# A range test moved into the second layer, and a shorter conversion of the weights

## The chip, the cores and the metric

The kernel runs on one core of a Trainium2 chip. The metric is the device time of one execution in microseconds (us), the median of several executions. The engines are named as the profile names them: PE is TensorE (its weight loads are PEld), DVE VectorE, ACT ScalarE, POOL GpSimd, and SP issues DMAs.

## What is computed

A linear attention with a decaying state, and after it two feed-forward layers with squared ReLU. Cut to what matters:

```python
def _attn_ref(r, k, v, w, u):            # (4, 8, 768, 48) each, u (8, 48)
    state = np.zeros((B, H, D, D))
    for t in range(S):
        cur = np.einsum('bhd,bhe->bhde', u[None] * kt, vt)
        y[:, :, t] = np.einsum('bhd,bhde->bhe', rt, state + cur)
        state = wt[:, :, :, None] * state + np.einsum('bhd,bhe->bhde', kt, vt)

def _moe_ref(x, w_in, w_out):            # x (3072, 384), w_in (384, 2048)
    r = np.maximum(x @ w_in, 0.0)
    return r * r @ w_out                 # twice, with two sets of weights
```

The decays `w` lie between 0.8 and 0.95. The weights come as 64-bit floats, two 32-bit words each, and the device turns them into 32-bit floats.

## The kernel before

Attention is cut into 24 tiles of 128 tokens (`tile_ops`, L168). For each tile DVE makes two scans over the decays, G from the back (`scan_g`, L223) and F from the front (`scan_f`, L229). The products of keys and queries with them (`scaled`, L253) go to PE: transposes `kb` (L265, for the first six tiles also sums at L268), scores `sc` (L296, 32 small matmuls), `U` (L321), the output `y` (L365) and its transpose `xp` (L375). DVE carries the state from tile to tile (`Sp` at L330, `Sn` at L340), adds at L370 and writes the low half of the result, `xl` (L386), after ACT has written the high half `xh` (L379). All of these results share three PSUM buffers, the tag `ab`, taken in turn: the n-th takes the one that the result three before it has given up. Each buffer is given up by the engine that copies it out: that of `kb` by ACT at L278, that of `sc` by ACT at L299, those of `U` by DVE at L340, that of `xp` by DVE at L386.

The kernel is exact only while the decays' products stay in range. So for each tile ACT squares G and F and sums them into one column of `chk` (L257). A general, slow program runs instead if a test fails; with these inputs it does not.

The feed-forward layers take the tokens in blocks (`BLOCKS`, L31: in layer 1 512, 256, 256 and four times 512 tokens, in layer 2 six times 512). For each of the 16 chunks of 128 hidden channels PE makes nine matmuls `h` (L695; three times three, since each operand is split into a high and a low half), ACT takes ReLU and square (L702, L707), the result is split into `gh` and `gl` (L714, L720), and nine matmuls go to `acc` (L738). The first `h` needs block 0 whole: the four tiles 0 to 3. Tiles 4 and 5 are made while PE works on block 0, and so on.

A chunk of weights (`chunk_ops`, L441) is loaded in 768 KB (L451, three buffers `raw`) and converted in six steps: ACT takes the magnitude of the high words, scaled, and sums it for a test (L456); DVE shifts it (L459), puts the sign in (L462) and the top three bits of the low words (L465); ACT rounds the high half `whi` (L469), DVE makes the low half `wlo` (L472). Layer 1's 16 chunks are converted before and during block 0, layer 2's at the end of layer 1 and in layer 2's first block, and all stay in SBUF for their layer.

A planner sets the order of instructions on each engine at build time (`Order`, L58). Every step has a cost in a table, the results it needs, the buffers it takes and gives back, and a due time; the planner always takes the step that can begin first, and among those that can begin within 0.1 the one due first. On the chip each engine then runs its instructions in that fixed order and waits for what is late. Where PE would be idle in the plan ahead of the first `h`, `keep_warm` (L639) puts in matmuls whose result nobody reads.

Of the kernel before, what the change touches and what calls it, by code (L numbers as in the profile page):

```python
# [129 lines left out]
class Attn:  # L130
# [34 lines left out]
    def bank(self):  # L165
        return self.ps.tile([128, 512], F32, tag="ab", name="ab")

    def tile_ops(self, order, i, due, xdst):  # L168
# [48 lines left out]
        def scan_g():  # L217
            GF = t["GF"] = self.wp1.tile([QR, 2, SW + 1], F32, tag="GF", name="GF")
            t["G"], t["F"] = GF[:, 0], GF[:, 1]
            aend = t["aend"] = self.wp.tile([QR, SEG], F32, tag="aend", name="aend", bufs=4)  # L220
            Wt = parts()[0]
            nc.vector.memset(self.starts[:, 65::65], 1.0)
            nc.vector.tensor_tensor_scan(out=t["G"][:, 1:][:, ::-1], data0=Wt[:, 1:][:, ::-1], data1=self.starts[:, 1:][:, ::-1],  # L223
                                         initial=0.0, op0=ALU.mult, op1=ALU.add)
            nc.vector.tensor_scalar(out=aend, in0=t["G"][:, 1:SW:65], scalar1=LEAST, scalar2=None, op0=ALU.max)  # L225
            nc.vector.reciprocal(out=self.starts[:, 0:SW:65], in_=aend)

        def scan_f():
            nc.vector.tensor_tensor_scan(out=t["F"][:, 1:], data0=parts()[0][:, 0:SW], data1=self.starts[:, 0:SW],  # L229
                                         initial=0.0, op0=ALU.mult, op1=ALU.add)  # L230
# [660 lines left out]
```

## Time and profile before

| | us |
|---|---|
| median of 3 runs | 943.89 |
| lowest and highest | 942.64, 943.93 |
| the profiled execution | 946.26 |
| its span, first to last instruction | 944.5 |
| PE busy in the span | 925.4 |
| DVE busy | 533.0 |
| ACT busy | 458.2 |

The profiled execution is 2.4 us above the median, and 1.8 us of it lie outside the span. PE is busy for 98% of the span, but matmuls are pipelined and a matmul at half clock is as busy as one at full clock, so the share alone doesn't say what can be saved. Before the first `h` its busy time is also filled up by the keep-warm matmuls.

### The profile page before, as it was taken

To read this page: it belongs to the slowest core of one execution; us is meant where nothing else is said; L and a number is where in the kernel's file an instruction comes from. 1 tells how busy PE (TensorE), PEld (TensorE's weight loads), DVE (VectorE), ACT (ScalarE), POOL (GpSimd) and SP (SyncE) were. 2 spreads that over 40 slices of the span, in tenths; PEclk is the share of its full clock that TensorE was granted. 3 is DMA by queue.
4 is the path that set the end of the run, shared out by engine and by line. 5 is a ranking of instruction groups with operands and counts; after the bars stand their busy time and mean duration, and the time that the engine had idled before them with its cause. 6 is when DMAs were issued, how large, how long until landed. Compare 5 with 4: busy or idle time off the path is not lost.

```text
span 944.5 us, 16077 instructions
## 1 busy us (share of the span) xinstructions
PE 925.4 (98%) x6392; PEld 782.6 (83%) x6392; DVE 533.0 (56%) x897; ACT 458.2 (49%) x850; POOL 106.8 (11%) x123
## 2 busy tenths in 40 slices
PE   7898999999999999999999999999999999999997
PEld 7887889998887888888888888888888888888896
DVE  6799888787758484664433999532422422422322
ACT  4667866676554654555343676432333333322331
POOL 2201304043404123030100000000000000000000
PEclk8798999999999999999999999999999999999999
DMA  9556423233313413131022453120110200200201
GB/s 244 144 163 216 157 78 105 83 110 118 105 52 95 123 53 93 34 98 45 1 86 82 155 194 130 40 52 0 37 31 1 49 19 0 56 1 1 35 1 37
DMA packets 57444, 73.78 MB, mean 78 GB/s; under 512 B 35888, under 2 KB 44208, under 8 KB 57360
## 3 DMA queue, kind: packets, MB, share of 16 engines
q1 hardware_dynamic: 56944, 72.27, 26.5%
q8 instruction: 52, 0.85, 0.4%
q10 hardware_dynamic: 416, 0.40, 0.1%
q14 instruction: 32, 0.26, 0.1%
HBM read 63.21 MB, written 9.44 MB: 77 GB/s over the span
## 4 chain that ended last, share of the span: by engine, by line
PE 76%; DVE 0%; DMA 0%; ACT 0%; issue 0%; ACTq 0%
PE acc L738 35%; PE h L695 35%; PE ab L365 2%; PE ab L296 1%; PE ab L321 1%; PE ab L265 1%; PE ab L375 0%; DMA out_dram<-o 0%; DVE GF L223 0%; DVE gh L714 0%; DVE aend L225 0%; DVE o L754 0%; ACT o L754 0%; DVE gl L720 0%; PE ab L400 0%
## 5 line engine op out<-in xcount | busy, mean ns | idle before, releaser
L702 ACT ACTIVATE gf<-h 128x512 f32<-128x512 f32 (+1 forms) x208 | 117.3, 564 | 346.5 <-PE h L695 319.7
L714 DVE CAST gh<-gf 128x512 fp32r<-128x512 f32 (+1 forms) x192 | 82.6, 430 | 329.9 <-PE acc L738 282.7
L695 PE MATMUL h<-xh,whi 128*128 128x512 f32 (+1 forms) x624 | 238.0, 381 | 0.0
L695 PE MATMUL h<-xl,whi 128*128 128x512 f32 (+1 forms) x624 | 234.1, 375 | 0.0
L695 PE MATMUL h<-xh,wlo 128*128 128x512 f32 (+1 forms) x624 | 233.9, 375 | 0.0
L738 PE MATMUL acc<-gh,whi 128*128 128x512 f32 (+1 forms) x576 | 217.7, 378 | 0.8 <-DVE gh L714 0.8
L738 PE MATMUL acc<-gl,whi 128*128 128x512 f32 (+1 forms) x576 | 214.3, 372 | 1.3 <-DVE gl L720 1.2
L738 PE MATMUL acc<-gh,wlo 128*128 128x512 f32 (+1 forms) x576 | 214.2, 372 | 0.0
L720 DVE TENSOR_TENSOR gl<-gf,gh 128x512 fp32r<-128x512 f32 (+1 forms) x208 | 144.8, 696 | 8.7 <-ACT gh L714 1.2
L695 PEld LDWEIGHTS h<-xh,wlo 128*128 128x128 f32 x624 | 117.9, 189 | 21.1
L695 PEld LDWEIGHTS h<-xh,whi 128*128 128x128 f32 x624 | 117.9, 189 | 21.1
L695 PEld LDWEIGHTS h<-xl,whi 128*128 128x128 f32 x624 | 118.0, 189 | 20.7 <-DVE xl L386 1.1
L707 ACT ACTIVATE gf<-gf 128x512 f32<-128x512 f32 (+1 forms) x208 | 124.6, 599 | 6.5
L738 PEld LDWEIGHTS acc<-gl,whi 128*128 128x128 f32 x576 | 108.6, 189 | 20.3 <-DVE gl L720 2.1
L738 PEld LDWEIGHTS acc<-gh,whi 128*128 128x128 f32 x576 | 108.6, 188 | 20.4 <-DVE gh L714 1.0
L738 PEld LDWEIGHTS acc<-gh,wlo 128*128 128x128 f32 x576 | 108.4, 188 | 18.9
L303 POOL TENSOR_SCALAR_AFFINE_SELECT rs<-rs 64x512 f32<-64x512 f32 x48 | 35.9, 749 | 300.9 <-ACT rs L299 299.3
L333 ACT COPY sv<-Sp 64x192 f32<-64x192 f32 x88 | 30.6, 348 | 42.5 <-DVE Sp L330 41.5
L223 DVE TENSOR_TENSOR_SCAN GF<-wkr,starts 112x520 f32<-112x520 f32 x24 | 31.9, 1329 | 5.4 <-DMA wkr<-in_wkr_dram 2.2
L253 DVE TENSOR_TENSOR wkr<-wkr,GF 112x512 f32<-112x512 f32 x48 | 33.8, 729 | 0.0
L472 DVE SCALAR_TENSOR_TENSOR wlo<-c,whi 128x768 fp32r<-128x768 f32 x32 | 30.7, 962 | 4.7 <-ACT whi L469 4.3
L465 DVE SCALAR_TENSOR_TENSOR c<-raw,c 128x768 int32<-128x768 int32 x32 | 31.6, 986 | 0.7
(67 smaller groups left out, 832.7 us busy)
## 6 DMA issues: line engine op xcount, KB each, us to landing
raw<-in_w_dram SPq DMA_DIRECT2D x32, 768.0 KB, 4.3
wkr<-in_wkr_dram SPq DMA_DIRECT2D x23, 675.9 KB, 6.6
rk<-in_nat_dram SPq DMA_DIRECT2D x18, 384.0 KB, 4.9
vn<-in_nat_dram SPq DMA_DIRECT2D x24, 192.0 KB, 2.6
sv<-in_nat_dram SPq DMA_DIRECT2D x48, 96.0 KB, 2.6
x<-o SPq DMA_DIRECT2D x15, 256.0 KB, 2.1
xr<-x SPq DMA_DIRECT2D x15, 256.0 KB, 2.6
out_dram<-o SPq DMA_DIRECT2D x120, 32.0 KB, 1.6
```

Source lines behind the costliest of these rows:

```text
L223: nc.vector.tensor_tensor_scan(out=t["G"][:, 1:][:, ::-1], data0=Wt[:, 1:][:, ::-1], data1=self.starts[:, 1:][:, ::-1], initial=0.0, op0=A ...
L253: nc.vector.tensor_tensor(out=x, in0=x, in1=seg(t["GF"[n]], 1 - n), op=ALU.mult)
L303: nc.gpsimd.affine_select(out=x, in_=x, pattern=[[0, SEG], [1, C]], base=0, channel_multiplier=-1, compare_op=ALU.is_gt, fill=0.0)
L333: nc.scalar.copy(out=t["sv"][own[a], a, c::2], in_=t["Sp"][own[a]])
L465: nc.vector.scalar_tensor_tensor(out=t["c"], in0=t["low"], scalar=29, in1=t["c"], op0=ALU.logical_shift_right, op1=ALU.bitwise_or)
L472: nc.vector.scalar_tensor_tensor(out=t["hl"][1], in0=t["cf"], scalar=BACK, in1=t["hl"][0].bitcast(F32), op0=ALU.mult, op1=ALU.subtract)
L695: nc.tensor.matmul(out=h[:, 0:N], lhsT=a[:, cs], rhs=b[:, kk, 0:N], start=n == 0, stop=n == 8)
L702: nc.scalar.activation(out=g[:, 0:N], in_=hs.pop((l, j, f))[:, 0:N], func=AF.Relu)
L707: nc.scalar.activation(out=g[:, 0:N], in_=g[:, 0:N], func=AF.Square)
L714: copy(out=gh[:, 0:N], in_=g[:, 0:N])
L720: nc.vector.tensor_tensor(out=gl[:, 0:N], in0=g[:, 0:N], in1=gh[:, 0:N].bitcast(F32), op=ALU.subtract)
L738: nc.tensor.matmul(out=dst, lhsT=a, rhs=c, start=f == n == 0, stop=f == KF - 1 and n == 2)
```

## The change

Three things. First, for tiles 0 to 5 the square on ACT goes away (`TESTED_LATE = 6`). Their decays are loaded again in layer 2, G and F are scanned again, and ACT squares them there (`Attn.test_ops`). Second, the conversion of a chunk has five steps: ACT makes an integer of the top three bits of the low word out of its top byte, in place (`tail`), DVE joins it with the shifted high word and masks the sign in (`join`, two steps), ACT rounds, DVE subtracts. It has no test in it. Third, the test of the weights is made in layer 2: every chunk of both layers is loaded a second time, ACT takes the magnitude, and DVE counts in two steps what is too large and what too small (`Weights.test_ops`); chunk k's magnitude waits for the second load of chunk k+1. The last steps on `chk` move from layer 2's second block to its last. Due times change as well: tiles 0 and 1, 2 and 3, and the weights (6 instead of 12 ahead of their use). `HALVED` is 0, so the new passes over half a block do not occur.

```diff
-SCALE, BACK, LARGEST = 2.0 ** -111, 2.0 ** -8, 2.0 ** -96
+TESTED_LATE = 6
+HALVED = 0
...
-            pe_y=1.14, pe_x=0.45, magnitude=1.1, shift=0.56, top=0.96, tail=0.96, hi=0.83, lo=0.96, issue=0.4, warm=0.3)
+            pe_y=1.14, pe_x=0.45, word=0.83, join=0.96, hi=0.83, lo=0.96, issue=0.4, warm=0.3)
...
+    def test_ops(self, order, i, due):
...
+        add("SP", C_["issue"], load, "w again", [("x", NTILE - 1)], take=[("wkr", key)], moves=4 * QR * SW)
+        add("DVE", C_["scan"] + C_["ends"], scan_g, "G again", [("w again", i), ("F again", i - 1) if i else ("F", NTILE - 1)], take=[("GF", key), ("aend", key)], port=True)
+        add("DVE", C_["scan"], scan_f, "F again", [("G again", i)], port=True)
+        add("ACT", C_["square"], lambda: self.sum_squares(t, i), "chk", [("F again", i)], drop=[("GF", key), ("aend", key), ("wkr", key)])
...
         for n in range(2):
-            add("DVE", C_["product"], lambda n=n: scaled(n), ("kS", "rT")[n], ["GF"[n], whole] + (["rkT"] if by_pe else []), 0.14, port=True)
-        add("ACT", C_["square"], lambda: nc.scalar.activation(out=t["GF"][:, :, 1:], in_=t["GF"][:, :, 1:], func=AF.Square, accum_out=self.chk[0:QR, i:i + 1]),
-            "chk", ["kS", "rT"], 0.16, drop=[("GF", i)])
+            add("DVE", C_["product"], lambda n=n: scaled(n), ("kS", "rT")[n], ["GF"[n], whole] + (["rkT"] if by_pe else []) + (["kS"] if n else []), 0.14, port=True,
+                drop=[("GF", i)] if n and i < TESTED_LATE else ())
+        if i >= TESTED_LATE:
+            add("ACT", C_["square"], lambda: self.sum_squares(t, i), "chk", ["kS", "rT"], 0.16, drop=[("GF", i)])
...
         def tail():
-            nc.vector.scalar_tensor_tensor(out=t["c"], in0=t["low"], scalar=29, in1=t["c"], op0=ALU.logical_shift_right, op1=ALU.bitwise_or)
+            low = t["raw"][:, :, 0]
+            nc.scalar.activation(out=low, in_=t["raw"].bitcast(U8)[:, :, 3], func=AF.Copy, scale=1 / 32, bias=-15.5 / 32)
+
+        def join(n):
+            low, high = t["raw"][:, :, 0], t["raw"][:, :, 1]
+            if n == 0:
+                t["c"] = self.tmp_p.tile([128, 2 * DM], I32, tag="c", name="c")
+                nc.vector.scalar_tensor_tensor(out=t["c"], in0=high, scalar=3, in1=low, op0=ALU.logical_shift_left, op1=ALU.bitwise_or)
+            else:
+                nc.vector.scalar_tensor_tensor(out=t["c"], in0=high, scalar=0x3FFFFFFF, in1=t["c"], op0=ALU.bitwise_or, op1=ALU.bitwise_and)
...
+    def test_ops(self, order, k, due, chk):
...
+        def size():
+            t["a"] = self.tmp_p.tile([128, 2 * DM], I32, tag="c", name="c").bitcast(F32)
+            nc.scalar.activation(out=t["a"], in_=t["raw"][:, :, 1].bitcast(F32), func=AF.Abs)
...
+        order.add("SP", C_["issue"], load, ("raw2", k), [("issued", ("raw2", k - 1) if k else ("raw", 2 * KF - 1))], due=due, early=EARLY, take=[("raw", ("test", k))], moves=2048 * DM)
+        add("ACT", "word", size, "size", [("raw2", min(k + 1, 2 * KF - 1))], take=[("c", ("test", k))])
+        add("DVE", "join", lambda: count(0), "count0", [("size", k)], port=True)
+        add("DVE", "join", lambda: count(1), "count", [("count0", k)], port=True, drop=[("c", ("test", k)), ("raw", ("test", k))])
...
-        lo, hi = (at[number[0, j - 1, 0]], at[number[0, j, 0]]) if j else (0, BEGIN)
-        lo, hi = lo + (hi - lo) * p / n, lo + (hi - lo) * (p + 1) / n
+        if j:
+            lo, hi = at[number[0, j - 1, 0] if j > 1 else HALVED], at[number[0, j, 0]]
+            lo, hi = lo + (hi - lo) * p / n, lo + (hi - lo) * (p + 1) / n
+        else:
+            lo, hi = ((0, BEGIN), (BEGIN * 0.8, at[HALVED]))[p]
...
-        W.chunk_ops(order, k, at[number[k // KF, 0, k % KF]] - 12, A.chk)
+        W.chunk_ops(order, k, at[number[k // KF, 0, k % KF]] - 6)
+    for i in range(TESTED_LATE):
+        A.test_ops(order, i, at[number[1, 1, 2 * i + 1]])
+    for k in range(2 * KF):
+        W.test_ops(order, k, at[number[1, 1 + k // 8, 2 * (k % 8)]], A.chk)
```

The new costs and due times make the planner set another order. It shows at three places ahead of and in block 0.

On DVE, where tile 3's decays and keys arrive (rows are line, instruction, what it writes and reads; the scans are listed as SCALAR_TENSOR_TENSOR). Before:

```order
L240 TENSOR_TENSOR rk<-wkr 112x512
L222 MEMSET starts 112x8
L223 SCALAR_TENSOR_TENSOR GF<-wkr,starts 112x520
L225 TENSOR_SCALAR aend<-GF 112x8
L226 RECIPROCAL starts<-aend 112x8
L386 TENSOR_TENSOR xl<-ab,xh 128x3x128
L229 SCALAR_TENSOR_TENSOR GF<-wkr,starts 112x520
L253 TENSOR_TENSOR wkr<-wkr,GF 112x512 x2
L330 TENSOR_TENSOR Sp<-Sn,aend 112x192
```

After:

```order
L180 SCALAR_TENSOR_TENSOR GF<-wkr,starts 112x520
L182 TENSOR_SCALAR aend<-GF 112x8
L183 RECIPROCAL starts<-aend 112x8
L186 SCALAR_TENSOR_TENSOR GF<-wkr,starts 112x520
L271 TENSOR_TENSOR rk<-wkr 112x512
L284 TENSOR_TENSOR wkr<-wkr,GF 112x512 x2
L503 SCALAR_TENSOR_TENSOR c<-raw,c 128x768
L418 TENSOR_TENSOR xl<-ab,xh 128x3x128
L179 MEMSET starts 112x8
L180 SCALAR_TENSOR_TENSOR GF<-wkr,starts 112x520
L182 TENSOR_SCALAR aend<-GF 112x8
```

The `xl` shown was tile 1's and stood inside tile 3's scans, with tile 0's ahead of them; now it is tile 0's and stands behind all of tile 3's scans and products, and tile 4's G follows at once (it stood after tile 3's state before).

On PE, from tile 3's transposes to its `U`. Before:

```order
L265 MATMUL ab<-ident,wkr 128x112 x4
L268 MATMUL ab<-ub,rk 128x2 x4
L296 MATMUL ab<-wkr 64x64 x16
L641 MATMUL h<-ident 128x128 x12
L321 MATMUL ab<-vn,ksT 64x48
```

After:

```order
L297 MATMUL ab<-ident,wkr 128x112 x4
L300 MATMUL ab<-ub,rk 128x2 x4
L328 MATMUL ab<-wkr 64x64 x16
L705 MATMUL h<-ident 128x128 x2
L353 MATMUL ab<-vn,ksT 64x48
```

Two keep-warm matmuls stand there instead of twelve. Ahead of tile 2's `U` there are 19 in a row instead of four, and that `U` takes the buffer of tile 0's `xp`.

On PE in block 0, at tile 5's transposes. Before:

```order
L321 MATMUL ab<-vn,ksT 64x48
L321 MATMUL ab<-vn,ksT 48x48
L265 MATMUL ab<-ident,wkr 128x112 x4
L268 MATMUL ab<-ub,rk 128x2 x4
L695 MATMUL h<-xh,whi 128x512
```

After:

```order
L772 MATMUL h<-xh,wlo 128x512
L297 MATMUL ab<-ident,wkr 128x112 x4
L300 MATMUL ab<-ub,rk 128x2 x4
L328 MATMUL ab<-wkr 64x64 x16
L772 MATMUL h<-xh,whi 128x512
```

Before, they came behind tile 4's `U` (two buffers) and so took the buffer of tile 4's scores; now they come ahead of it, behind the fourth `h`, and tile 5's scores follow them at once.

## Rows read from the trace of the kernel before

**Rows 1.** Stretches: start:end, length, busy PE, PEld, DVE, ACT, POOL, clock, DMA, GB/s.
```profile
35.80:46.00 10.20, 9.13 (x66) 9.02 (x67) 7.95 (x13) 6.96 (x14) 1.73 (x3) 0.50 0.28 93
...
73.40:80.20 6.80, 6.64 (x22) 5.78 (x23) 6.11 (x7) 3.12 (x8) 1.93 (x2) 0.50 0.71 205
...
31.07:55.48 24.41, 21.01 (x261) 19.18 (x257) 19.90 (x35) 13.61 (x28) 4.34 (x6) 0.79 0.46 130
55.48:134.65 79.17, 76.20 (x499) 62.14 (x499) 72.44 (x99) 60.75 (x109) 11.54 (x10) 0.96 0.49 161
134.65:240.00 105.35, 103.75 (x1235) 98.00 (x1234) 81.43 (x162) 69.33 (x159) 29.78 (x34) 1.00 0.34 101
...
640.00:680.00 40.00, 40.00 (x178) 33.15 (x177) 13.03 (x24) 13.32 (x22) 0.00 (x0) 1.00 0.05 14
```

**Rows 2.** Timeline of PE before block 0: start, length, instruction, [idle before <-releaser].
```profile
34.51 0.66 PE L321 MATMUL ab<-vn,ksT 64*64 64x48 f32 x28 [0.15 <-DVE xl L386]
...
36.87 0.98 PE L265 MATMUL ab<-ident,wkr 112*128 112x112 f32 x4 [1.28 <-issue]
...
39.31 1.98 PE L296 MATMUL ab<-wkr 48*64 48x64 f32 x32
41.22 5.24 PE L641 MATMUL h<-ident 128*128 128x128 f32 x24
46.38 0.68 PE L321 MATMUL ab<-vn,ksT 64*64 64x48 f32 x32
...
55.48 0.47 PE L695 MATMUL h<-xh,whi 128*128 128x512 f32 x1
```

**Rows 3.** Timeline of DVE before block 0, the same columns.
```profile
31.07 0.69 DVE L240 TENSOR_TENSOR rk<-wkr 112x512 f32<-112x512 f32 x1 [1.04 <-DMA wkr<-in_wkr_dram]
...
37.30 0.34 DVE L330 TENSOR_TENSOR Sp<-Sn,aend 112x192 f32<-112x192 f32 x1
...
43.30 0.36 DVE L330 TENSOR_TENSOR Sp<-Sn,aend 112x192 f32<-112x192 f32 x1 [1.28 <-ACT sv L333]
...
47.10 0.36 DVE L340 TENSOR_TENSOR Sn<-ab,Sp 112x192 f32<-112x192 f32 x1 [1.71 <-PE ab L321]
```

**Rows 4.** Timeline of PE in block 0, around tile 5's transposes.
```profile
64.71 0.39 PE L695 MATMUL h<-xh,whi 128*128 128x512 f32 x1
...
66.75 0.55 PE L265 MATMUL ab<-ident,wkr 112*128 112x112 f32 x4
...
67.96 0.47 PE L738 MATMUL acc<-gh,whi 128*128 128x512 f32 x1
...
73.56 1.01 PE L265 MATMUL ab<-ident,wkr 112*128 112x112 f32 x4 [2.46 <-ACT rs L299]
...
75.95 0.77 PE L695 MATMUL h<-xh,whi 128*128 128x512 f32 x1
...
79.94 0.52 PE L738 MATMUL acc<-gh,whi 128*128 128x512 f32 x1
```

**Rows 5.** Groups by form on DVE: instruction, count | busy us, mean ns | idle.
```profile
L465 DVE SCALAR_TENSOR_TENSOR c<-raw,c 128x768 int32<-128x768 int32 x32 | 31.6, 986 | 0.7
...
L472 DVE SCALAR_TENSOR_TENSOR wlo<-c,whi 128x768 fp32r<-128x768 f32 x32 | 30.7, 962 | 4.7 <-ACT whi L469 4.3
L229 DVE TENSOR_TENSOR_SCAN GF<-wkr,starts 112x520 f32<-112x520 f32 x24 | 30.2, 1257 | 0.2
...
L459 DVE TENSOR_SCALAR c<-c 128x768 int32<-128x768 int32 x32 | 17.7, 552 | 0.0
...
L386 DVE TENSOR_TENSOR xl<-ab,xh 128x384 fp32r<-128x384 f32 x24 | 13.1, 547 | 0.6 <-ACT xh L379 0.6
```

**Rows 6.** Groups by form on ACT, the magnitude of a chunk, the same columns.
```profile
L456 ACT ACTIVATE c<-raw 128x768 f32<-128x768 f32 x32 | 29.0, 906 | 4.4 <-DVE wlo L472 3.9 <-DVE starts L222 0.4
```

**Rows 7.** Timeline of a stretch in layer 2, DVE and PE.
```profile
643.65 0.69 DVE L720 TENSOR_TENSOR gl<-gf,gh 128x512 fp32r<-128x512 f32 x1
...
649.04 0.39 PE L738 MATMUL acc<-gh,whi 128*128 128x512 f32 x1
```

More of the change, by code (lines that the diff above doesn't have):

```diff
@@ L215, in parts @@
             return w[:, 0:SW + 1], *(w[:, SW + 1 + 512 * n:SW + 513 + 512 * n].rearrange("q (s t) -> q s t", s=SEG) for n in range(2))
[L217 to L230, printed above, removed]
+        scan_g, scan_f = self.scans(t)
         add("DVE", C_["scan"] + C_["ends"], scan_g, "G", ["w"] + ([("F", i - 1)] if i else []), 0.0, take=[("GF", i), ("aend", i)], port=True)
@@ L446, in add @@
         def add(engine, what, run, gives, needs=(), **kw):
-            order.add(engine, C_[what], run, (gives, k), [n if isinstance(n, tuple) else (n, k) for n in needs], due=due, early=EARLY, **kw)
+            order.add(engine, C_[what], run, (gives, k), [(n, k) for n in needs], due=due, early=EARLY, **kw)
         def load():
-            t["raw"] = self.raw_p.tile([128, 2 * DM, 2], I32, tag="raw", name="raw")
-            nc.sync.dma_start(out=t["raw"], in_=self.packed[k // KF][k % KF].bitcast(I32).rearrange("p (m w) -> p m w", w=2))
@@ L467, in hi @@
         def hi():
             t["hl"] = self.hl[k // KF, k % KF] = tuple(self.p.tile([128, 2 * DM], F32R, tag=n, name=n) for n in ("whi", "wlo"))
-            nc.scalar.activation(out=t["hl"][0], in_=t["cf"], func=AF.Copy, scale=BACK)
+            nc.scalar.copy(out=t["hl"][0], in_=t["c"].bitcast(F32))
         def lo():
-            nc.vector.scalar_tensor_tensor(out=t["hl"][1], in0=t["cf"], scalar=BACK, in1=t["hl"][0].bitcast(F32), op0=ALU.mult, op1=ALU.subtract)
-        add("SP", "issue", load, "raw", [("issued", ("raw", k - 1))] if k else [], take=[("raw", k)], moves=2048 * DM)
@@ L475, in chunk_ops @@
-        add("ACT", "magnitude", magnitude, "abs", ["raw"] + ([("abs", k - 1)] if k else []), take=[("c", k)])
-        add("DVE", "shift", shift, "shift", ["abs"], port=True)
-        add("DVE", "top", top, "top", ["shift"], port=True)
-        add("DVE", "tail", tail, "tail", ["top"], port=True, drop=[("raw", k)])
-        add("ACT", "hi", hi, "whi", ["tail"] + ([("whi", k - 1)] if k else []), take=[("w", k)])
-        add("DVE", "lo", lo, "wlo", ["whi"], port=True, drop=[("c", k)])
+            nc.vector.tensor_tensor(out=t["hl"][1], in0=t["c"].bitcast(F32), in1=t["hl"][0].bitcast(F32), op=ALU.subtract)
@@ new lines, in chunk_ops @@
+        order.add("SP", C_["issue"], load, ("raw", k), [("issued", ("raw", k - 1))] if k else [], due=due, early=EARLY, take=[("raw", k)], moves=2048 * DM)
+        order.add("ACT", C_["word"], tail, ("tail", k), [("raw", k)] + ([("tail", k - 1)] if k else []), due=due, early=EARLY)
+        add("DVE", "join", lambda: join(0), "join0", ["tail"], take=[("c", k)], port=True)
+        add("DVE", "join", lambda: join(1), "join", ["join0"], port=True, drop=[("raw", k)])
+        order.add("ACT", C_["hi"], hi, ("whi", k), [("join", k)] + ([("whi", k - 1)] if k else []), due=due, early=EARLY, take=[("w", k)])
```

139 lines of the change are left out of this document (88 added, 51 removed).

## Prediction

> **What bounds the kernel now.** I read the busy times by stretch first [rows 1]. In layer 2 PE is busy without a gap, at full clock, and DVE and ACT work 13 of 40 us each: nothing but PE counts there. From 134.65 to 240 PE is idle for 1.6 us in all. What is left lies ahead of that. From tile 3's data (31.07) to the first `h` (55.48) PE's busy time is mostly filling, and DVE works 19.90 of 24.41 us. In block 0, from 55.48 to 134.65, PE has about 3 us of gaps and a mean clock of 0.96. So the time is the start of the first `h`, plus PE's work from there, plus what gaps and half clock cost in block 0. Then I read the timelines of PE and DVE ahead of the first `h` [rows 2, 3] and of PE around the largest gap in block 0 [rows 4].
>
> **The change part by part.**
>
> *Up to tile 3's data, nothing.* DVE gets tile 3's data at 31.07 after a wait for its DMA [rows 3]. The loads queued ahead of it are the same ones, in nearly the same order. The squares that leave ACT would let the buffer go a little earlier, but the transfer waits behind others, so I cost this at nothing. If the queue were not full, it would bring up to the 1.04 us of that wait.
>
> *The first `h`.* It needs `xl` of tile 3, the last of a row of DVE instructions. I compare DVE's list from 31.07 to there, before and after. Chunk 0 loses the shift and two bit steps and keeps one join, since its first join moves ahead of 31.07: 0.55 + 0.99 + 0.99 - 0.99 = 1.54 us less. Chunk 1 loses its shift, 0.55. Chunk 2 gets its second join into the stretch for the shift: 0.99 - 0.55 = 0.44 more. Tile 0's `xl` comes in, 0.55, and tile 4's F scan, 1.26 [rows 5]. Together 0.16 more, so 20.1 us of DVE work after 19.90. If DVE never waited, the first `h` would start at 51.2; with all the 4.5 us of waiting that DVE has now, at 55.6.
>
> The two largest of the old waits are 1.28 us at 43.30, for ACT's copy of tile 2's state, and 1.71 us at 47.10, for tile 3's `U` [rows 3]. Both come from PE at half clock (granted 0.50 from 35.8 to 46.0) [rows 1]: the scores of tile 3 took 1.9 us there, and twelve keep-warm matmuls took 5.2 us ahead of that `U` [rows 2]. The new order has two keep-warms in that place. But it brings a wait of its own. Tile 2's `U` takes the buffer of tile 0's `xp`, which DVE gives up with tile 0's `xl`, and that now stands behind tile 3's scans, products and a join. Tile 3's scans and products with one `xl` between them took from 31.07 to 37.30 [rows 3]; with a join more they end at about 38.2. So tile 2's `U` runs at about 38.2 instead of 34.51 [rows 2], with PE idle or filling before. Queued behind it on PE are all of tile 3's matmuls.
>
> From there the path depends on the clock. At half clock: `U` 1.36 (twice the 0.68 of row 46.38), tile 3's transposes and sums 2.44 (36.87 to 39.31), scores 1.91 (39.31 to 41.22), two keep-warms 0.87 (5.24 / 12 each, the 24 rows of that line being two for each), `U` 1.36 [rows 2]: 7.9 us, so tile 3's `U` ends at 46.1. DVE then has four instructions for tile 3's state (0.36 each), two `xl` besides tile 3's own and two sums of about the same length, tile 4's F 1.26, one low half of weights 0.96, chunk 2's joins 1.98 and tile 3's `xl` 0.55 [rows 3, 5]: 8.4 us, and the first `h` starts at 54.5. At full clock PE has the transposes in 1.21 (66.75 to 67.96) [rows 4] and the rest in about half, tile 3's `U` is there before DVE asks for it, and the first `h` starts at 51.2 to 51.8. The stretch in which PE has only 19 keep-warms ends in several us without work, and in the old trace an idle time of 2.46 us was followed by half clock [rows 1, 4]. So I stand nearer to the half-clock end, at 53.3: **2.2 us earlier**, with ends of 4.3 earlier and 0.1 later (the old waits back in full).
>
> *Block 0.* Tile 5's transposes waited 2.46 us for the buffer of tile 4's scores, which ACT had yet to copy [rows 4]. PE's clock then stood at half from 73.4 to 80.2 [rows 1]: transposes and sums took 2.39 us (73.56 to 75.95) instead of 1.21, the next `h` 3.99 (75.95 to 79.94) instead of 2.04 (64.71 to 66.75) [rows 4]: 1.18 + 1.95 = 3.1 us. In the new order these transposes come ahead of tile 4's `U` and take a buffer that is long free; tile 5's scores take that of tile 4's transposes, which ACT gives up with one copy. That takes 2.46 + 3.1 = 5.6 us away. What is late next is the weights: every `h` of block 0 needs its chunk, and DVE works 72.44 of these 79.17 us [rows 1]. The change takes one shift of 0.55 per chunk away from DVE, about 8 us in the block, so this wait should be smaller than the old one, not larger. The order of the two chunks converted side by side can still cost one `h` a wait; no row shows it, so its bounds are 0 and the old gap of 2.46, and if it is long enough 3.1 of half clock with it. I take 0.8, a third of the gap, since DVE's load falls. **4.8 us less**, between 5.6 less and 0.
>
> *The new byte step on ACT* reads a byte and writes an integer, and no row shows it. The nearest is the magnitude with its strided read, 0.91 us [rows 6]; twice that is the upper end. ACT works 13.61 of the 24.41 us ahead of the first `h` and 60.75 of 79.17 in block 0, and has lost the magnitude for it, so either end is hidden.
>
> *From 134.65 on.* Nothing is taken away, the tiles' order shifts a little: 0, within 1.6 us either way, the idle time now [rows 1].
>
> *Layer 2.* The tests add 38 loads, 38 steps on ACT, 64 counts and 12 scans on DVE, from the end of its first block on, after the last conversion. Per two chunks of the feed-forward (8.2 us) these are at most 0.9 us on ACT, 2 us of counts and, for the first six, 2.5 us of scans (twice 1.26) on DVE, where 27 of 40 us are free [rows 1]. `gl` ends at 644.34 and its matmuls start at 649.04 [rows 7]: 4.7 us in which one such step may stand ahead. I cost it at nothing. Without that cover each step would cost PE its length.
>
> **Sum.** -2.2 - 4.8 = -7.0 us. The profiled execution of before is 946.26, with a span of 944.5 that would become 937.5; the median of the runs is 943.89, which gives **936.9**.
>
> **The rivals.**
>
> *The clock falls once more in block 0.* A wait for weights or buffers that is short by itself is followed by one stretch at half clock: 3.1 us of the gain come back, 936.9 + 3.1 = 940.0. For it: one gap did that before [rows 4]. Against: DVE and ACT both have less to do there. The Trainium skill (TensorE: Matmul & The Clock Gate, What's actually happening) says the opposite of such terms: "the ramp penalty is <1% of a typical kernel span", not to be fitted. By that the clock would be left out of block 0, the gain there would be the gap alone, and the time again about 940. The trace agrees with the size, 3.1 of 944 us, but that is as much as the gap itself, so I keep it in the sum.
>
> *Both gains are lost.* The old waits come back ahead of the first `h` (55.6), and the gap only moves to another result in block 0: 943.9, no change. For it: three buffers are still shared by all the tiles' results.
>
> *Slower, by tile 2's `U`.* It waits for tile 0's `xl`, PE goes quiet, and the half clock lasts until the first `h`: besides the 3.3 us up to 46.1 that this path is late against the full clock, the outputs `y` and `xp` of tiles 2 and 3 also run at half clock and DVE waits for each. With two more waits of the old size (1.28 + 1.71 = 3.0) on top of 54.5 the first `h` starts at 57.5, 2 us late; with the block 0 gap moved, 946. It decides if the first `h` comes later than 55.5 and a gap of 2.4 us or more remains in block 0.
>
> *The tests are not hidden.* ACT stands at a magnitude whose load has not landed, with ReLU queued behind it, for longer than the 4.7 us; at 0.4 us for each of 32 loads that is 13 us, 950. Against: the loads are issued well ahead, and in layer 2 the DMA engines are nearly idle (0.05) [rows 1].
>
> **How the numbers follow.** Forecast 0.55 (about 933.5 to 939), half clock once more 0.20, both lost 0.13, slower by `U` 0.07, tests not hidden 0.05. The low end takes the start 4.3 us earlier, 5.6 in block 0 and little else: -10, 933.5. The high end, 943.5, takes in the second case and the near part of the third; what is left out is about 2 in 10. A difference of 0.2%, 1.9 us, is about what a measurement of this kernel can tell from no change. Faster 0.75, same 0.13, slower 0.12.
>
> **What would show it.** The first `h` starts between 51 and 54.5 instead of at 55.48. In block 0 no wait of tile 5's transposes for a copy on ACT, and a clock of 1.00 from about 60 on; block 0 takes some 74 to 75 us instead of 79.2. Tile 2's `U` starts near 38, with a wait for DVE's `xl`. In layer 2 PE stays without gaps. I am wrong if tile 3's data come at another time, if the clock stays at half into block 0, if an `h` of block 0 waits for `wlo`, or if ACT's ReLU in layer 2 is late for PE.

## The result, and the profile after

The changed kernel is slower: a median of 953.37 us (951.81 to 957.76) against 943.26 us of before (940.72 to 943.93), a ratio of 1.0124 with a 95% interval of 1.0106 to 1.0141 (the ratios here are those on record; they need not be the quotient of the two medians, which is 1.0107). Its profiled execution has a span of 951.2 us, 6.7 us more than that of before.

The starts of the blocks, read from the timelines of PE at the first `h` of each, show that the two halves of the kernel went opposite ways (how much of the first difference is the change's own comes further down):

| first `h` of | before | after | difference |
|---|---|---|---|
| layer 1, block 0 | 55.48 | 50.92 | -4.56 |
| layer 1, block 1 | 134.65 | 124.78 | -9.87 |
| layer 1, block 2 | 178.84 | 170.62 | -8.22 |
| layer 2, block 0 | 540.56 | 532.41 | -8.15 |
| layer 2, block 1 | 605.84 | 597.69 | -8.15 |
| layer 2, block 2 | 671.48 | 668.66 | -2.82 |
| layer 2, block 3 | 736.76 | 735.49 | -1.27 |
| layer 2, block 4 | 802.04 | 805.08 | +3.04 |
| layer 2, block 5 | 867.32 | 873.22 | +5.90 |

Up to layer 2's second block the gain is there, 8.15 us. Then four blocks, the ones beside which the tests run, lose 14.05 us of it and more: 275.53 us instead of 261.48. The last block is another 0.8 longer, for a reason that is open; most of it, 0.6, is there without the tests too.

The page's busy times and its chain of waits for after:

```profile
PE 925.3 (97%) x6386; PEld 779.7 (82%) x6386; DVE 585.7 (62%) x1023; ACT 479.7 (50%) x850; POOL 104.0 (11%) x123
...
PE 27%; SPq 4%; DMA 2%; DVE 1%; issue 1%; ACT 0%; DVEq 0%; ACTq 0%
PE h L772 13%; PE acc L810 13%; SPq L835 4%; DMA xr<-x 2%; DMA wkr<-in_wkr_dram 1%; DVE raw L538 0%; DVE o L823 0%; DMA out_dram<-o 0%; ACT gf L778 0%; SPq L479 0%; DVE gl L793 0%; DVE GF L180 0%; DVE gh L788 0%; DVE xl L892 0%; DVE o L826 
```

In a kernel that PE bounds, a share for SP's queue in the chain (L835, the output stores of layer 2, and behind them `xr`, the loads of layer 2's input) is the first hint. The stretches of after answer [rows 1]: the same bounds at work, up to the first `h`, block 0, the rest up to 240, then four blocks of layer 2 one by one.

```profile
35.80:46.00 10.20, 10.14 (x121) 9.31 (x120) 7.26 (x15) 6.55 (x13) 2.85 (x3) 0.52 0.43 151
31.07:50.92 19.85, 17.92 (x225) 16.29 (x225) 16.77 (x29) 10.56 (x20) 4.38 (x4) 0.74 0.44 137
50.92:124.78 73.86, 72.29 (x494) 58.51 (x493) 64.57 (x87) 56.75 (x92) 11.69 (x10) 1.00 0.50 171
124.78:240.00 115.22, 114.00 (x1337) 105.38 (x1336) 84.52 (x164) 74.11 (x166) 31.94 (x39) 1.00 0.38 111
...
597.69:668.66 70.97, 67.44 (x289) 55.14 (x288) 48.86 (x95) 32.92 (x54) 0.00 (x0) 0.98 0.39 122
668.66:735.49 66.83, 65.57 (x289) 53.98 (x288) 35.85 (x70) 27.34 (x44) 0.00 (x0) 1.00 0.38 118
735.49:805.08 69.59, 66.98 (x289) 55.06 (x288) 35.93 (x70) 27.49 (x44) 0.00 (x0) 0.98 0.37 114
805.08:873.22 68.14, 65.58 (x289) 53.99 (x288) 36.20 (x74) 26.76 (x43) 0.00 (x0) 1.00 0.26 77
```

Block 0 is at full clock and PE has 1.6 us of gaps in it, where it had 3. In layer 2, where PE had no gap [rows 1], it now has 1.3 to 3.5 us of gaps per block, and in the first and third of the four the clock is below full. DVE is idle for 31% of the first of the four and for nearly half of the others, ACT for more than half of each.

**One stall, read step by step.** In the block that begins at 735.49, SP's queue, ACT, PE, and PE's clock show where it comes from. First the DMA issues on SP (start, length, line, transfer, count):

```profile
739.30 0.33 SPq L885 DMA_DIRECT2D xr<-x  x1
743.24 12.52 SPq L835 DMA_DIRECT2D out_dram<-o  x24
755.80 0.45 SPq L479 DMA_DIRECT2D raw<-in_w_dram  x1
756.35 0.38 SPq L885 DMA_DIRECT2D xr<-x  x1
```

The 24 output stores of the block before (three parts, 8 DMAs each, L835) occupy SP for 12.52 us. The planner counts 0.4 us for a part, 1.2 in all. Behind them stand a second load of weights (L479) and then the last of the three loads of the next block's input, `xr` (L885). The landing times of L885 from 735 to 775, of which the longest is that load's, and ACT's timeline:

```profile
DMA to landing us min/median/max: 2.7/2.7/5.2
```

```profile
752.30 0.90 ACT L533 ACTIVATE c<-raw 128x768 f32<-128x768 f32 x1
761.58 0.62 ACT L894 CAST xh<-xr 128x512 fp32r<-128x512 f32 x1 [8.38 <-DMA xr<-x]
762.10 0.59 ACT L778 ACTIVATE gf<-h 128x512 f32<-128x512 f32 x1
```

ACT is at its next step, the split of that input (L894), at 753.2 and stands there for 8.38 us. The ReLU behind it (L778), whose `h` had long been ready, comes at 762.10. PE waits for it, and then runs at half clock:

```profile
762.75 0.80 PE L772 MATMUL h<-xh,whi 128*128 128x512 f32 x1 [2.61 <-ACT gf L778]
```

```profile
762.40:765.80 3.40, 3.05 (x7) 2.50 (x8) 2.87 (x6) 2.87 (x5) 0.00 (x0) 0.50 0.53 178
```

The same block of before takes 65.28 us, and PE is busy for all of it:

```profile
736.76:802.04 65.28, 65.28 (x290) 54.07 (x288) 21.80 (x39) 21.32 (x35) 0.00 (x0) 1.00 0.11 25
```

Here PE is busy for 66.98 us, 1.70 more, with a stretch of 3.40 us at the 1.2 GHz level in it. The gap of 2.61 and these 1.70 make 4.31 us, and that is what the block loses: 69.59 less 65.28.

In that block of before, SP had issued the second and third load of the next block's `xr` ahead of its stores:

```profile
737.44 5.77 SPq L811 DMA_DIRECT2D xr<-x  x2
744.50 12.94 SPq L763 DMA_DIRECT2D out_dram<-o  x24
```

In after's block at 597.69 there is a second wait of the same kind: a tile's second load (`wkr`, L201) also stands behind the stores, and DVE at its scan, with `gh` and `gl` queued behind it, so that PE waits for 3.29 us:

```profile
623.86 1.24 DVE L180 TENSOR_TENSOR_SCAN GF<-wkr,starts 112x520 f32<-112x520 f32 x1 [7.65 <-DMA wkr<-in_wkr_dram]
```

```profile
627.66 0.49 PE L810 MATMUL acc<-gh,whi 128*128 128x512 f32 x1 [3.29 <-DVE gh L788]
```

ACT stands at the split there too, for 6.49 us up to 624.25, but the scan and two counts behind it on DVE last longer, up to 627.19. This block loses 5.69 us of the four blocks' loss, the other three 1.55, 4.31 and 2.86. So an old load and a new one are late for the same reason, the stores ahead of them on SP's queue.

**The start.** PE's timeline ahead of the first `h`, in the places of [rows 2]:

```profile
32.92 0.68 PE L353 MATMUL ab<-vn,ksT 64*64 64x48 f32 x32
35.16 0.86 PE L297 MATMUL ab<-ident,wkr 112*128 112x112 f32 x4 [1.56 <-DVE starts L179]
...
37.61 1.98 PE L328 MATMUL ab<-wkr 48*64 48x64 f32 x32
39.52 1.22 PE L705 MATMUL h<-ident 128*128 128x128 f32 x4
40.67 1.10 PE L353 MATMUL ab<-vn,ksT 64*64 64x48 f32 x32
...
50.92 0.47 PE L772 MATMUL h<-xh,whi 128*128 128x512 f32 x1
```

DVE's first work on tile 3, which was the row of 31.07 in [rows 3], and its waits after that, where [rows 3] had 1.28 and 1.71:

```profile
28.36 1.24 DVE L180 TENSOR_TENSOR_SCAN GF<-wkr,starts 112x520 f32<-112x520 f32 x1 [1.31 <-DMA wkr<-in_wkr_dram]
...
41.60 0.36 DVE L362 TENSOR_TENSOR Sp<-Sn,aend 112x192 f32<-112x192 f32 x1 [0.59 <-ACT sv L365]
...
43.15 0.56 DVE L418 TENSOR_TENSOR xl<-ab,xh 128x384 fp32r<-128x384 f32 x1 [0.73 <-ACT xh L411]
...
45.87 0.56 DVE L402 TENSOR_TENSOR ys<-ab,vn 128x384 f32<-128x384 f32 x1 [0.90 <-PE ab L397]
```

Tile 3's data reach DVE 2.71 us earlier. Tile 3's `U` is at 40.67 instead of 46.38, at half clock, and no wait of DVE between the data and the first `h` is over 1 us. In block 0, tile 5's transposes, the row of 73.56 in [rows 4], have no wait at all:

```profile
66.35 0.55 PE L297 MATMUL ab<-ident,wkr 112*128 112x112 f32 x4
```

The new steps cost what was expected of them: the byte step on ACT, the first join on DVE, one count (all by form, mean ns last but one):

```profile
L495 ACT ACTIVATE raw<-raw 128x768 int32<-128x768 uint8 x32 | 29.0, 908 | 2.5 <-DMA raw<-in_w_dram 2.3
```

```profile
L538 DVE SCALAR_TENSOR_TENSOR raw<-c 128x768 f32<-128x768 f32 x64 | 58.4, 951 | 0.0
...
L501 DVE SCALAR_TENSOR_TENSOR c<-raw 128x768 int32<-128x768 int32 x32 | 32.5, 1016 | 2.6 <-ACT raw L495 2.5
```

### The profile page after: what moved, and what is told of

Same layout as the page of the kernel before. It is cut to its first block, busy times and chain, and to the rows that moved or that the text cites. A ratio compares the mean times of both kernels' runs of the same rounds, so it can differ in the third digit from the quotient of the medians.

```text
span 951.2 us, 16197 instructions
## 1 busy us (share of the span) xinstructions
PE 925.3 (97%) x6386; PEld 779.7 (82%) x6386; DVE 585.7 (62%) x1023; ACT 479.7 (50%) x850; POOL 104.0 (11%) x123
## 5 line engine op out<-in xcount | busy, mean ns | idle before, releaser
L778 ACT ACTIVATE gf<-h 128x512 f32<-128x512 f32 (+1 forms) x208 | 117.2, 564 | 296.5 <-PE h L772 262.9
L788 DVE CAST gh<-gf 128x512 fp32r<-128x512 f32 (+1 forms) x192 | 80.1, 417 | 259.8 <-PE acc L810 168.7
L793 DVE TENSOR_TENSOR gl<-gf,gh 128x512 fp32r<-128x512 f32 (+1 forms) x208 | 147.8, 710 | 12.7 <-ACT gh L788 5.1
L772 PEld LDWEIGHTS h<-xh,wlo 128*128 128x128 f32 x624 | 117.8, 189 | 22.5 <-DVE wlo L510 1.4
L538 DVE SCALAR_TENSOR_TENSOR raw<-c 128x768 f32<-128x768 f32 x64 | 58.4, 951 | 0.0
L180 DVE TENSOR_TENSOR_SCAN GF<-wkr,starts 112x520 f32<-112x520 f32 x30 | 38.3, 1276 | 17.4 <-DMA wkr<-in_wkr_dram 12.4
L186 DVE TENSOR_TENSOR_SCAN GF<-wkr,starts 112x520 f32<-112x520 f32 x30 | 37.3, 1242 | 0.2
L320 ACT COPY rs<-wkr 64x512 f32<-64x512 f32 (+1 forms) x48 | 29.3, 612 | 9.7 <-issue 4.3
```

Source lines behind the costliest of these rows:

```text
L186: nc.vector.tensor_tensor_scan(out=t["F"][:, 1:], data0=t["wkr"][:, 0:SW], data1=self.starts[:, 0:SW], initial=0.0, op0=ALU.mult, op1=ALU.add)
L538: nc.vector.scalar_tensor_tensor(out=out, in0=a, scalar=(HIGHEST, LOWEST)[n], in1=a, op0=(ALU.is_gt, ALU.is_lt)[n], op1=ALU.mult, accum_ou ...
L772: nc.tensor.matmul(out=h[:, 0:N], lhsT=a[:, cs], rhs=b[:, kk, o:o + N], start=n == 0, stop=n == 8)
L778: nc.scalar.activation(out=g[:, 0:N], in_=hs.pop((l, j, f, o))[:, 0:N], func=AF.Relu)
L788: copy(out=gh[:, 0:N], in_=g[:, 0:N])
L793: nc.vector.tensor_tensor(out=gl[:, 0:N], in0=g[:, 0:N], in1=gh[:, 0:N].bitcast(F32), op=ALU.subtract)
```

## The experiments: layer 2

Theory 1 is the reading above: the x2 load (the load of layer 2's input into `xr`) is queued behind 24 stores. Theory 2: the second loads' bytes crowd the DMA engines. Theory 3: the tests' own work on ACT and DVE delays ReLU.

**Without the tests (e1_no_tests).** The loops over `test_ops` in `chunked` go, and the flag no longer needs their results:

```diff
-    for i in range(TESTED_LATE):
-        A.test_ops(order, i, at[number[1, 1, 2 * i + 1]])
-    for k in range(2 * KF):
-        W.test_ops(order, k, at[number[1, 1 + k // 8, 2 * (k % 8)]], A.chk)
```

> The changed kernel without any of the tests in layer 2 (the second loads, magnitudes and counts of the weights, the second loads and scans of the first six tiles are left out, so weights and tiles 0 to 5 go untested; everything else is as changed). All theories: the start stays as in the changed kernel (first h near 50.9, block 1 near 124.8, layer 2 near 532.4), each block of layer 2 takes 65.3 us again as before the change, the time is about 8 us less than before, 934 to 936. If the loss in layer 2 has another cause than the tests, the time stays above 943.

Measured: 937.84 us, ratio to before 0.9948 (0.9932 to 0.9964), span 936.8. Blocks 1 to 4 of layer 2 take 261.12 us, 65.28 each. So the whole loss is the tests', and what is ahead of layer 2 is a gain, of 4.9 us between the medians. The time is 2 us above what I expected: I had taken the 8.15 us of the two profiles for the medians' gain.

**The planner told of the stores' length (e2_stores_planned_long).**

```diff
-    ... COST["issue"], lambda l=l, j=j, m=m: store(l, j, m), ...
+    ... 4.1 if l == 1 and by_channel(l, j) else COST["issue"], lambda l=l, j=j, m=m: store(l, j, m), ...
```

> The changed kernel with one planner's cost changed: the issue of a store of layer 2 counts 4.1 us (12.3 us for three, as the trace shows), not 0.4. All tests stay. Theory 1 (24 stores fill SP's queue for 12 us, the x2 load planned right behind them lands late, ACT stands at the split of x2 with ReLU behind it): the planner now places the split of that part 3 to 8 slots of 4.1 us later, so nearly all of the 14 us of stalls in layer 2 go and the time is 935 to 939. Theory 2 (25 MB more on the DMA engines slow the loads) and theory 3 (the tests' work on ACT and DVE itself is what delays ReLU): the stalls stay, 948 to 954.

Measured: 937.98 us, 0.9954 (0.9942 to 0.9966). The four blocks take 261.12 us. All tests are there, all bytes, all steps; SP's order is still stores first, x2 load behind them, but ACT's split now stands later and waits 0.7 us in sum. Theories 2 and 3 alone are out.

**The stores on another queue (e5_stores_pool).** L835 issues from POOL, which has nothing else to do in layer 2; the planner's step moves to it.

```diff
-                    nc.sync.dma_start(out=dst.rearrange("(s t) c -> t s c", t=32), in_=src)
+                    nc.gpsimd.dma_start(out=dst.rearrange("(s t) c -> t s c", t=32), in_=src)
```

> The changed kernel with the 24 output stores of each block of layer 2 issued from POOL's queue instead of SP's; the tests and the orders of ACT, DVE and PE stay. Theory 1 (the x2 load stands behind the stores in SP's queue): the third x2 load of a block lands 8 to 12 us sooner, ACT's wait at the split falls from 30 us in sum to under 8, blocks 1 to 4 of layer 2 take 65.3 us again, 935 to 939. Should POOL's own issue be much slower than the 0.5 us of SP, the buffers of the stored sums come free later and ReLU waits for those instead. Theory 2 (bytes) and theory 3 (work of the tests): the stalls stay, 948 to 954.

Measured: 937.38 us, 0.9944 (0.9924 to 0.9963), the four blocks again 261.12 us. POOL needs longer for a store than SP (582 ns against 449, medians), but no wait for that costs time. The waits from 590 to 945, after first, then this kernel:

```profile
ACT xh L894 <- DMA xr<-x: 30.1, 5, 8.4
ACT gf L778 <- DMA out_dram<-o: 24.3, 5, 6.8
```

```profile
ACT gf L778 <- DMA out_dram<-o: 25.5, 6, 6.4
...
ACT xh L894 <- DMA xr<-x: 0.9, 2, 0.6
```

(Columns: engine, line, what it waited for, us in sum, times, longest.) The wait for x2 is gone. The other one, of ReLU for a buffer that a store must first have read, is as long as it was: 6.4 to 6.8 us, and it costs nothing.

**Small tests in the same order (e3_small_tests).** The second loads of the weights, magnitudes and counts on 96 of 768 columns (so most of that test is left out):

```diff
-            t["raw"] = self.raw(k)
+            nc.sync.dma_start(out=t["raw"][:, 0:96], in_=...[:, 0:96])
...
-            nc.scalar.activation(out=t["a"], in_=t["raw"][:, :, 1].bitcast(F32), func=AF.Abs)
+            nc.scalar.activation(out=t["a"][:, 0:96], in_=t["raw"][:, 0:96, 1].bitcast(F32), func=AF.Abs)
```

> The changed kernel with each second load of a weight chunk, its magnitude and its counts cut to 96 of 768 columns; number, order and places of all instructions stay (most of the weights' test is left out). Theories 2 and 3: with an eighth of the bytes and of the work, the loss of layer 2 is gone, about 936. Theory 1: the stores and the order in SP's queue stay, the last x2 load of a block comes some 2 us sooner for the smaller load ahead of it, ACT still waits for it 3 to 6 us in each of four blocks, and 4 to 12 us of the 14 us stay: 940 to 949.

Measured: 940.52 us in one run, span 938.3, the four blocks 262.71 us. Less than theory 1 said (4 to 12 us), more than the others (nothing): 1.6 us are left of the 14. So the size of the tests matters too. This edit cuts their bytes and their work together; what points at the bytes is how soon the x2 load lands. ACT's waits, in sum 23.3 us:

```profile
ACT xh L895 <- DMA xr<-x: 23.3, 5, 6.8
```

In the block of the stall above the x2 load lands 2.6 us after its issue here; with the 768 KB load issued just ahead of it, it took 5.2.

**Before, with the order alone (e4_before_x2_behind).** One need added, so that the third x2 load of blocks 2 to 5 comes behind the stores; no tests:

```diff
-    ("x2", j, m), [...] + ([chain] if chain else [("x", NTILE - 1)])
+    ("x2", j, m), [...] + ([chain] if chain else [("x", NTILE - 1)]) + ([("stored", 1, j - 2, 2)] if m == 2 and j > 1 else [])
```

> The kernel before the change, with one need added: from block 2 of layer 2 on, the third x2 load of a block is issued after the stores of the block two before it. No tests, no other bytes. Theory 1: the load is queued behind 24 stores (12 us), ACT stands at the split of x2 for some 5 to 8 us in four blocks, ReLU is late, and the time is 8 to 16 us above before, 951 to 960. Theories 2 and 3: order alone costs nothing, 943 to 945.

Measured: 940.87 us in one run, span 939.1. Theory 1 as I had put it is wrong here: the waits come as expected, and the time doesn't. The four blocks take 261.85 us, 0.4 more than before:

```profile
ACT xh L820 <- DMA xr<-x: 22.5, 4, 6.4
```

A wait of up to 6.4 us is free here, then. The slack that I see for it: ACT waits for PE for some 2.7 us in each slot of 4.1 anyway, PE has a second buffer for `h`, and `gl` is 4.7 us ahead of its matmuls [rows 7]. That the order alone uses this up and no more is argued from these rows; no run varies the slack.

**A little beyond (e8_behind_plus_8).** The kernel above with eight small loads more ahead of the third x2 load:

```diff
+        if m == 2 and j > 1:
+            for n in range(8):
+                nc.sync.dma_start(out=spare[32 * (n % 4):32 * (n % 4) + 32, n // 4], in_=x2[0][0:32, 0, 0:512].rearrange("p (s c) -> p s c", c=64)[:, :, 0:16])
```

> The kernel e4_before_x2_behind with eight small loads more (of the stores' form, 32 partitions by 8 pieces, read into a tile that nobody uses) ahead of the third x2 load of blocks 2 to 5. If ACT's wait at the split is free up to some 6.5 us (22.5 us in four waits cost 0.4 us there) and costs beyond that: the waits grow by about 3.6 us to 9 to 10 us each, each of four blocks loses 3 to 5 us and more where the clock falls to half, 953 to 962. If waits of that length at the split cost nothing by themselves: 941 to 944.

Measured: 966.4 us in one run, span 964.7; the four blocks take 285.39 us, 23.5 more than without the eight loads, which occupy SP for 3.90 us per block. That is more than the 962 at most that I expected: PE is busy 11.3 us longer than the 261.12 of four blocks without a loss, at half clock after each of the four gaps, and idle for 13.0. ACT, PE and the clock in one of the blocks:

```profile
771.02 0.62 ACT L824 CAST xh<-xr 128x512 fp32r<-128x512 f32 x1 [9.82 <-DMA xr<-x]
```

```profile
772.18 0.80 PE L695 MATMUL h<-xh,whi 128*128 128x512 f32 x1 [3.56 <-ACT gf L702]
```

```profile
771.00:775.00 4.00, 2.81 (x7) 2.24 (x8) 2.80 (x5) 2.86 (x5) 0.00 (x0) 0.50 0.19 66
```

Put together, by the longest wait at the split:

| kernel | longest wait | sum | blocks 1 to 4 of layer 2 |
|---|---|---|---|
| after, stores on POOL | 0.6 | 0.9 | 261.12 |
| after, stores planned long | 0.7 | 0.7 | 261.12 |
| after, no tests | 1.2 | 5.5 | 261.12 |
| before | 1.5 | 5.2 | 261.48 |
| before, x2 behind the stores | 6.4 | 22.5 | 261.85 |
| after, small tests | 6.8 | 23.3 | 262.71 |
| after | 8.4 | 30.1 | 275.53 |
| before, x2 behind stores and 8 loads | 10.4 | 38.4 | 285.39 |

There is an edge near 6 us, though not at one sharp value. Wait by wait, PE has no gap over 0.25 us behind the 4.86 to 6.38 us of before with x2 behind the stores. With small tests a wait of 5.72 us gives a gap of 0.55, one of 6.79 gives 0.40, and 5.88 none. In after 7.12, 7.20 and 8.38 us give 1.26, 2.56 and 2.61, and with the eight loads 8.44 to 10.36 us give 2.74 to 3.59. Below the edge the wait is free; above it most of each us is lost, and in the longer stalls part of that again at half clock. The row of after also holds the 5.69 us of its first block, where DVE's wait for a tile's second load ended last.

The 12 us of stores bring the x2 load to the edge, and the tests' loads ahead of it push it over. Alone they cost 0.4 us (order) and nothing (tests on a free queue). That it is the stores on SP's queue is shown twice, by moving them and by planning with their length; how the 14 us divide between the x2 loads and the tile's second load is read from one profile.

## The experiments: the start and block 0

Two parts of the change act there: the squares of six tiles that leave ACT, and the new conversion with its due times. Theory A says the second makes the gain (block 0 by PE's order and the lighter DVE), theory B the first.

**Squares back (e6_squares_back)**, in the kernel without tests:

```diff
-TESTED_LATE = 6
+TESTED_LATE = 0
```

> The kernel e1_no_tests with the squares of the first six tiles back on ACT in the attention part, so only the conversion of the weights and the planner's due times are the changed ones (the weights go untested). PE's order in block 0 is that of the changed kernel (tile 5's transposes ahead of tile 4's U), with squares. Theory A (block 0 gains by that order and by the shift taken from DVE): block 0 takes 74 to 75 us, as in the changed kernel (73.9). Theory B (it gains by the squares that left ACT): block 0 takes 77 to 79 us, as before. Whole time 935 to 938 by A, 939 to 942 by B.

**Squares out (e7_before_no_squares)**, in the kernel before (tiles 0 to 5 go untested there):

```diff
-        add("ACT", C_["square"], lambda: nc.scalar.activation(out=t["GF"][:, :, 1:], ...), "chk", ["kS", "rT"], 0.16, drop=[("GF", i)])
+        if i >= 6:
+            add("ACT", C_["square"], lambda: nc.scalar.activation(out=t["GF"][:, :, 1:], ...), "chk", ["kS", "rT"], 0.16, drop=[("GF", i)])
```

> The kernel before with the squares of the first six tiles left out (those tiles go untested) and nothing in their place; the old conversion and, in block 0, the old order of PE stay. Theory A (order and conversion): block 0 takes 77 to 79 us as before, 942 to 944. Theory B (squares): block 0 takes 74 to 75 us, 937 to 940.

Measured: 941.15 and 938.72 us, one run each, with block 0 at 73.26 and 76.51 us. Block 0 follows theory A (76.51 is close to the 76.56 at full clock in another profile of the start of before), while the two times lean to B. The reason is the first `h`, at 53.91 in the first and 50.36 in the second, and what one profile says of that was not to be trusted, as the kernel before with x2 behind the stores had just shown: its start is before's, instruction for instruction, and its first `h` came at 50.92, not at 55.48. So all four corners were timed on one chip, with the repaired kernel beside them.

> The kernel of e6_squares_back once more (new conversion and order, squares of the first six tiles on ACT, no tests in layer 2), now timed, in a table of two by two with before, e10 and e11. If the gain ahead of layer 2 is the conversion's and the order's alone: ratio 0.994 to 0.996, as e11. If the squares that left ACT bring the first h forward: 0.997 to 0.999, 2 to 4 us behind e11.

> The kernel of e7_before_no_squares once more (before without the squares of the first six tiles, which go untested), now timed. If the gain ahead of layer 2 is the conversion's and the order's: ratio 0.999 to 1.001. If it is the squares': 0.994 to 0.997.

> The kernel of e1_no_tests once more (conversion, order and squares changed, no tests in layer 2), as the fourth cell of the table: 0.994 to 0.996, by every theory.

> The kernel of e5_stores_pool once more, the whole changed kernel with the stores of layer 2 on POOL's queue, as the version to keep. If the tests then cost nothing, as I predicted of the changed kernel, it equals e11: 0.994 to 0.996, with a difference between the two under 0.1%. If a part of their cost stays, it is 1 to 3 us slower than e11.

| kernel | median, us | ratio to before | interval |
|---|---|---|---|
| before | 942.55 | 1 | |
| squares out | 941.65 | 0.9990 | 0.9974 to 1.0007 |
| new conversion and order | 939.73 | 0.9972 | 0.9959 to 0.9984 |
| both, no tests | 938.82 | 0.9959 | 0.9941 to 0.9977 |
| the whole change, stores on POOL | 938.59 | 0.9957 | 0.9943 to 0.9971 |

The conversion and its order bring 2.8 us of the 3.7; the squares' 0.9 can't be told from nothing. Theory A holds for the squares out alone (0.999 to 1.001 expected). The new conversion alone, 0.9972, lies inside what B had said (0.997 to 0.999), with an interval that reaches into A's 0.994 to 0.996. So the larger part is the conversion's and the order's, and a share of the squares in the first `h` is not excluded. The last row is the version to keep: it has every test of the changed kernel, these cost nothing that could be measured (0.9957 against 0.9959 without them), and it is faster than both kernels.

What the profiles of all these runs show of the start:

| start as in | profiles | first `h` | mean granted clock, 15 to 48 us | block 0 |
|---|---|---|---|---|
| before | 3 | 50.92, 54.17, 55.48 | 0.90, 0.74, 0.74 | 77.64, 76.56, 79.17 |
| before, squares out | 2 | 49.82, 50.36 | 0.84, 0.84 | 76.46, 76.51 |
| new conversion, squares in | 2 | 50.80, 53.91 | 0.84, 0.74 | 73.31, 73.26 |
| after | 7 | 48.03 to 51.33 | 0.79 to 0.90 | 73.82 to 73.88 |

The first `h` varies by up to 4.6 us from one execution to the next of the same start. Two things vary with it. One is the clock: among profiles of one start before the change, and of the new conversion with the squares in, the later first `h` goes with the lower clock (among the seven of after it does not always). The stretch from 15 to 48 in before, then in before with x2 behind the stores:

```profile
15.00:48.00 33.00, 27.31 (x382) 25.65 (x380) 24.33 (x40) 19.73 (x40) 9.89 (x12) 0.74 0.68 187
```

```profile
15.00:48.00 33.00, 27.32 (x430) 25.29 (x431) 29.38 (x48) 22.33 (x45) 11.38 (x12) 0.90 0.72 200
```

The other is the load of tile 3's decays, which landed at 31.05 in before and at 27.96 and 27.70 in the two other profiles of its start. Whether the clock is the cause, or fell because the work came late, is not shown.

## Why the prediction was wrong, point by point

*Layer 2: "I cost it at nothing" failed.* This is the step that turned the sign: 14.05 us. I had weighed the tests as steps on ACT and DVE against the free time of these engines and the 4.7 us ahead of `gl`'s matmuls [rows 7]. That was right as far as it went: the counts took 0.95 us, and in the kernel with the stores on POOL all the steps together cost nothing, though the "0.9 us on ACT" had left out the squares of the six tiles, 1.07 us each. What I did not do was walk SP's queue. The tests' steps stand in the planner's order ahead of the x2 chain, the third x2 load slips behind the stores, and the stores hold SP for 12 us where the planner thinks 1.2. In the first of the four blocks the second load of a tile, one of the tests' own, stood behind the stores as well, and 5.69 of the four blocks' loss are there. The prediction had named the sign, ACT's ReLU in layer 2 late for PE, and it came. All of that could be read beforehand: 24 stores of half a us each are in the trace of before, with the x2 loads just ahead of them, and the new order of SP's instructions could be laid beside it.

*The rival "the tests are not hidden"* had the right shape and the wrong instruction: "ACT stands at a magnitude whose load has not landed, with ReLU queued behind it". ACT stood at the split of x2, which was in the kernel already; the new loads only delayed it. I had spoken against it with idle DMA engines. The queue that was full was SP's, not theirs. Its 950 us was near the 953 for a reason that isn't the one given, and 0.05 was too little.

*Up to tile 3's data, nothing:* not so in this pair of profiles. DVE's first work on tile 3 begins at 28.36 (now the scan, after a wait of 1.31 us for the load) instead of 31.07, so 2.71 of the 4.56 us lie ahead of the stretch that the forecast was about, and the prediction's own sign of being wrong, data at another time, came true. It need not be the change that did it: with x2 behind the stores, a kernel with the start of before, DVE begins tile 3 at 28.37 and does not wait:

```profile
28.37 0.68 DVE L240 TENSOR_TENSOR rk<-wkr 112x512 f32<-112x512 f32 x1
```

*The first `h`:* forecast 53.3, between 51.2 and 55.6; it came at 50.92, in the other six profiles of this start at 48.03 to 51.33, so below the range in six of seven. Counted from DVE's first work on tile 3, the way to the first `h` takes 22.56 us instead of 24.41, with 19.38 us of DVE's work where the list had 20.1: 1.85 less against the forecast 2.2. But in the kernel just named, with the old start, it takes 22.55. So this pair can't show a gain of the new order there, and that 2.2 is near 1.85 is luck. PE ran at half clock from 35.8 to 46 here as in before, and the first `h` came early all the same. One step in it was wrong: tile 2's `U` did not wait for tile 0's `xl` and run near 38.2, it ran at 32.92; the wait for that `xl` came one result later, at tile 3's transposes, and took 1.56 us (the row names the memset right behind the `xl`). And its base was off: 55.48 was the latest of the three profiles of that start. So the rival of a slow start by tile 2's `U` did not come up (its 3.3 us "up to 46.1" are really 54.5 less 51.2, the lateness of the first `h`; by the same rows PE's way up to 46.1 would be 4.0 us longer at half clock). Nor did that of the clock falling once more or that of both gains lost: block 0 is at full clock, and without layer 2's loss a gain stands in the medians.

*Block 0:* forecast 74 to 75 us, measured 73.86, with the wait of tile 5's transposes gone and the clock at 1.00, as said. But two terms of it were mis-sized. Six output matmuls (two groups of three) moved to block 1, which is 45.84 us long instead of 44.19, so 1.65 of the gain is only moved. And the 3.1 us of half clock belonged to one execution, not to the order. In the kernel with x2 behind the stores the gap is the same 2.46 us, and the transposes behind it run at full clock:

```profile
68.98 0.60 PE L265 MATMUL ab<-ident,wkr 112*128 112x112 f32 x4 [2.46 <-ACT rs L299]
69.42 0.96 PE L268 MATMUL ab<-ub,rk 112*128 112x2 f32 x8
```

There the clock fell 2 us later, and block 0 takes 77.64 us; in the profile with the eight loads more, after the same gap of 2.46 (72.25), it stayed at 1.00, and block 0 takes 76.56. So the term of 3.1 was 2.6 in before (79.17 less 76.56), 1.1 in one execution and nothing in another. Against the block 0 at full clock the change gains 2.70 us, and 1.05 without the 1.65 that only moved: that 4.8 came out near 5.3 is luck.

The Trainium skill (TensorE: Matmul & The Clock Gate, What's actually happening) advises against fitting a model to a particular count of slow matmuls; by that rule, as the prediction worked it out, the gain would have been 3.9 us and the time 940, and the kernels without stalls in layer 2 measured 3.7 to 4.9 us under before. Ahead of layer 2 the rule gave the better size, though the terms left in that sum were not measured one by one. In layer 2 it would not do: there half clock was 1.7 of the 4.31 us of one stall.

*From 134.65 on, 0 within 1.6:* the start of layer 2 is 8.15 us earlier against 9.87 at block 1, and after the 1.65 moved to block 1 no block up to there differs by more than 0.3.

*Sum:* forecast 7.0 us less. Without layer 2's loss it is 8.15 less in the two profiles, but 3.7 (0.9959) in medians. The sum was made against one execution, and I had taken its start for the program's. Of the forecast 7.0 us the medians of the kernels without stalls show 3.7 to 4.9.

## What to carry to other kernels

When a change adds loads, lay the new order of the issuing queue beside the old one and cost each issue at its traced length, and see which old load has slipped behind what: a load is late by all that is issued ahead of it, and an engine that works in order hands that wait to whatever stands behind. Such a wait is free up to an edge (here some 6 us), so a kernel can stand right at it without a sign; ask of every hidden wait how far it is from costing. And before a term is taken from one profile, look at whether another execution of the same part shows it.

## What the runs showed of the hardware

A store of 32 KB in pieces of 128 bytes occupies SP's queue for 0.45 us (median) and POOL for 0.58, so 24 of them take 12 and 14 us, on SP with the DMA engines mostly idle (DMA share 0.11 from 590 to 945 before the change). On POOL they overlap with SP's loads, and the four blocks take the 261.12 us of the kernel without tests. The Trainium skill (Perfetto Trace Analysis, DMA Optimizations) recommends in general what repaired this kernel, one issuing engine for inputs and another for outputs; here the runs agree: 1.0124 for the changed kernel with one queue, 0.9957 with two.

A load of 256 KB that lands 2.6 us after its issue took 5.2 when a load of 768 KB had been issued just ahead of it on the same queue.
